# A pre-norm linear-attention and GEGLU block: nearly all matmuls as 64-row pairs, and a new order on every engine

## The chip, the cores and the metric

The kernel runs on one core of one Trainium2 chip. A core has TensorE (matmuls, from SBUF into the eight banks of PSUM), VectorE, ScalarE and GpSimd for elementwise work, and queues that issue transfers; here SyncE's queue (SP) issues nearly all of them, and ScalarE's the first three. The metric is the device time of one execution in microseconds, the median of several runs. A profile is one execution of its own; its span, from the first to the last instruction, is a little shorter than its time.

## The reference

All tensors are bf16; x has 2048 rows (tokens) of 448 values.

```python
def _A_ref(x, wqkv, wo):            # 16 heads of 28 values
    qkv = (x @ wqkv) ...            # wqkv: 448 x 1344
    phi = lambda t: jnp.where(t > 0, t + 1, jnp.exp(t)) + 1e-6
    pq, pk = phi(q), phi(k)
    kv = jnp.einsum("bhsd,bhse->bhde", pk, v)
    z = jnp.einsum("bhsd->bhd", pk)
    num = jnp.einsum("bhqd,bhde->bhqe", pq, kv)
    den = jnp.einsum("bhqd,bhd->bhq", pq, z)[..., None] + 1e-6
    return (num / den) ... @ wo     # wo: 448 x 448

h  = x + _A_ref(_layernorm(x), wqkv, wo)
n  = _layernorm(h)
h2 = h + (gelu(n @ w_gate) * (n @ w_up)) @ w_down    # 448 x 1792, 448 x 1792, 1792 x 448
```

The sums kv and z run over all tokens. So no output of attention can begin before the last token has been added, while Q needs only its own tokens.

## The kernel before, in words

**Tiles.** The 2048 tokens are 16 tiles of 128. The width of 448 is 3.5 times 128, or 7 times 64. A matmul takes a block of weights of up to 128 rows (the contracted dimension) and up to 128 columns, and streams up to 512 columns of data past it. It may also use only the upper or the lower 64 rows of the array; two such matmuls, one on each half, that write different PSUM banks form a pair.

**Stages and names.** Each task has a name and a number; the names return in the prediction.

- Warm-up: warm0 (38 matmuls on 128 rows), warm1 (8 pairs).
- First norm: for each tile statistics and aggregate (bnst, bnag) on VectorE, the inverse deviation on ScalarE (ln, rstd), the normalised rows (norm), on VectorE for tiles 0 and 1 and on GpSimd for the rest, there with a negated mean (negm). The rows are transposed into `xnT`: tiles 0 to 3 on TensorE (tr) with a copy from PSUM (ev), the others by transposing transfers (xT), for which ScalarE repeats the last 64 columns (dup).
- kv, per one or two tiles: k takes three 128-row matmuls, v takes three, and then v adds the last 64 rows of both as one pair. phi(k) is an exponential on ScalarE (ek), a clamp on GpSimd (cl) and a combination on VectorE (ph); v is copied by ScalarE (evv). acc adds four groups of 112 columns with a column of ones into one PSUM bank (`BK_ACC`). After the last tile VectorE masks the sum into `kvz` (kz1, kz2).
- Q: 16 groups, (four stretches of 512 tokens) x (four groups of 112 columns). qp takes four 128-row matmuls, of which the lower half of the last is zeros; then exponential (eq, ScalarE), clamp (cq, GpSimd) and combination from PSUM (pq, VectorE) into `pqT`.
- Attention's output, per tile: nd (four matmuls, 113 rows), reciprocal and product (rd, om) on VectorE, a transposition (tro and a copy evo for tiles 0 and 1, a transposing transfer oT for the others), wo, the residual and the second norm's statistics (hr, hbnst, hbnag) on VectorE, the norm (hln, hrstd, normh), a repetition of columns (wrap) and a transposition (trh and evh, or hT).
- GEGLU: gate/up groups gu0 to gu55, in chunks of 2, 2, 4, 4 and 4 tiles. Each is a run of 64-row pairs, gate on the upper rows into bank 0 or 1, up on the lower into bank 6 or 7. ScalarE applies the gelu (ge, two halves), VectorE multiplies (hm, two halves). down multiplies 14 blocks of 128 rows per tile; VectorE adds the residual (out) and a transfer stores it (dout).

**Order.** Nothing is scheduled at run time. `ORDERS` holds for TensorE, ScalarE, VectorE, GpSimd and SP one list of task names, and each engine works through its own list. A task that needs another engine's result, or a buffer that is still read, waits by semaphore; everything behind it in its list waits too. `_Graph.add` finds these dependences from the buffers that a task reads and writes, the PSUM banks among them; with `mw=True` a task places each wait in front of the matmul that needs it. In the lists, the last tasks of TensorE are down8 to down15; tile 15 is split in two halves of columns. Arguments such as `dur`, `lat`, `key` and the constants at the top served the search for an order and issue nothing.

The matmul of one Q group, and the end of v, read:

```python
for k in range(4):
    ins = e.matmul(psQ, wq_sb[:, k, g * GW:(g + 1) * GW], xnT[:, k, c * QCH:(c + 1) * QCH], start=(k == 0), stop=(k == 3))
...
ins = e.matmul(ps[:, BK_K[t % 4], 0:D], xnT[0:64, 3, t * 128:(t + 1) * 128], wt_sb[0:64, :], start=False, stop=True)
ins = e.matmul(ps[:, BK_V[t % 2], 0:D], xnT[64:128, 3, t * 128:(t + 1) * 128], wt_sb[64:128, :], start=False, stop=True)
```

Of the kernel before, what the change touches and what calls it, by code (L numbers as in the profile page):

```python
# [875 lines left out]
```

## Time and profile before

| | |
|---|---|
| median of 3 runs | 200.32 us (200.12 to 201.09) |
| the profiled execution | 200.7 us |
| its span | 199.0 us |
| TensorE's clock | 1.000 |
| busy: TensorE, VectorE, ScalarE, GpSimd | 97%, 60%, 36%, 25% of the span |

A line of a group names the source line, the engine, the operation, the tiles written and read, the shape (partitions x elements) and the count; then the busy time in us and the mean duration of one in ns; then the idle time before it and what ended it. In a timeline the first number is the start in us and the second the time from the first start to the last end of what is merged in the row. PE is TensorE, PEld its weight loads, DVE VectorE, ACT ScalarE, POOL GpSimd.

### The profile page before, as it was taken

Reading aid. Unit: us, or ns where it says so; the run is one execution under the profiler, and the core shown is the slowest. Engines: PE = TensorE matmul, PEld = TensorE weight load, DVE = VectorE, ACT = ScalarE, POOL = GpSimd, SP = SyncE. Lnnn points to the kernel's source line nnn. Section 1 sums busy time; section 2 is a strip of 40 time slices with the busy share of each in tenths; the row PEclk is TensorE's granted clock in tenths of the full one; section 3 lists DMA queues with packets and bytes.
Section 4 is the critical chain, followed back from the end, with each engine's and each line's share of the span. In section 5 each row is a group of like instructions: output and inputs, shape, how many; then the busy total and the mean of one; then the engine's idle time right before and its main releaser. Section 6 shows DMA issues by size and latency. Waiting matters only on the chain.

```text
span 199.0 us, 4435 instructions
## 1 busy us (share of the span) xinstructions
PE 193.8 (97%) x1698; PEld 113.6 (57%) x1698; DVE 119.5 (60%) x301; ACT 72.3 (36%) x203; POOL 50.6 (25%) x104
## 2 busy tenths in 40 slices
PE   7999999999998999999999999999999999999995
PEld 7544554566596865784454545665545455645554
DVE  3898434299999959497784877544513354442212
ACT  3487683665662330224310334344410243410000
POOL 2299973464315052241050235000000000000000
DMA  6974536996760532555226202700000100001111
GB/s 195 377 227 85 105 54 131 235 241 127 212 180 14 110 63 46 118 80 122 48 45 149 53 3 48 138 3 2 3 19 28 46 3 0 0 3 46 46 46 46
DMA packets 37172, 17.41 MB, mean 87 GB/s; under 512 B 28256, under 2 KB 36256, under 8 KB 37152
## 3 DMA queue, kind: packets, MB, share of 16 engines
q1 hardware_dynamic: 36272, 16.39, 34.8%
q10 hardware_dynamic: 880, 0.75, 1.2%
q8 instruction: 13, 0.21, 0.5%
q14 instruction: 7, 0.06, 0.1%
HBM read 8.66 MB, written 1.84 MB: 53 GB/s over the span
## 4 chain that ended last, share of the span: by engine, by line
PE 89%; DVE 4%; DMA 2%; ACT 2%; POOL 1%; issue 1%; DVEq 0%; POOLq 0%
PE ps L774 30%; PE ps L735 21%; PE ps L776 11%; PE ps L610 5%; PE ps L548 4%; PE ps L556 4%; PE ps L673 4%; DMA oT<-o_sb 2%; PE ps L440 2%; PE ps L585 2%; PE ps L634 2%; PE ps L559 2%; DVE pqT L615 1%; PE ps L674 1%; ACT xnT L527 1%; DVE o_sb L638 1%
## 5 line engine op out<-in xcount | busy, mean ns | idle before, releaser
L776 PE MATMUL ps<-hnT,wgu_sb 64*128 64x512 bf16 (+1 forms) x490 | 87.0, 334 | 0.0
L774 PE MATMUL ps<-hnT,wgu_sb 64*128 64x512 bf16 (+1 forms) x490 | 86.7, 333 | 0.0
L798 ACT ACTIVATE gl<-ps 128x256 bf16<-128x256 f32 x112 | 36.9, 381 | 82.1 <-PE ps L776 79.3
L800 DVE TENSOR_TENSOR hh<-ps,gl 128x256 bf16<-128x256 f32 x112 | 42.6, 418 | 28.5 <-ACT gl L798 26.1
L774 PEld LDWEIGHTS ps<-hnT,wgu_sb 64*128 64x128 bf16 x490 | 45.3, 94 | 20.9 <-issue 0.7
L776 PEld LDWEIGHTS ps<-hnT,wgu_sb 64*128 64x128 bf16 x490 | 43.9, 94 | 9.9 <-DVE hh L800 2.9
L735 PE MATMUL ps<-wd_sb,hh 128*128 128x448 bf16 (+1 forms) x238 | 43.3, 342 | 0.0
L735 PEld LDWEIGHTS ps<-wd_sb,hh 128*128 128x128 bf16 x238 | 22.9, 98 | 19.5 <-issue 1.0
L740 DVE TENSOR_TENSOR x_sb<-ps,x_sb 128x448 bf16<-128x448 f32 (+1 forms) x17 | 10.1, 594 | 24.2 <-PE ps L735 24.2
L456 DVE BATCH_NORM_STATS2 st<-x_sb 128x6 f32<-128x448 bf16 x32 | 18.8, 613 | 2.4 <-DMA x_sb<-in_A_x_dram 2.3
L577 DVE SCALAR_TENSOR_TENSOR pk<-ps,tm 128x448 bf16<-128x448 f32 x16 | 9.3, 621 | 11.2 <-POOL tm L575 9.6
L610 PE MATMUL ps<-xnT,wq_sb 128*112 128x512 bf16 x64 | 15.9, 380 | 0.0
L614 POOL TENSOR_SCALAR tm<-e 112x512 bf16<-112x512 bf16 x16 | 9.9, 621 | 9.2 <-ACT e L613 7.3
L615 DVE SCALAR_TENSOR_TENSOR pqT<-ps,tm 112x512 bf16<-112x512 f32 x16 | 10.7, 681 | 1.8 <-POOL tm L614 1.8
L613 ACT ACTIVATE e<-ps 112x512 bf16<-112x512 f32 x16 | 9.6, 600 | 4.7 <-PE ps L610 4.4
L548 PE MATMUL ps<-wkv_sb,xnT 128*128 128x448 bf16 x48 | 10.6, 353 | 0.2 <-ACT xnT L527 0.2
L575 POOL TENSOR_SCALAR tm<-e 128x448 bf16<-128x448 bf16 x16 | 8.8, 561 | 7.4 <-ACT e L574 7.4
L684 DVE TENSOR_TENSOR x_sb<-ps,x_sb 128x448 bf16<-128x448 f32 x16 | 9.4, 619 | 2.1 <-PE ps L675 2.1
L556 PE MATMUL ps<-wkv_sb,xnT 128*128 128x448 bf16 x48 | 10.6, 353 | 0.0
L698 POOL TENSOR_SCALAR hn<-x_sb,nm,rs 128x448 bf16<-128x448 bf16 x14 | 10.3, 745 | 0.8
L579 ACT ACTIVATE v<-ps 128x448 bf16<-128x448 f32 x16 | 8.7, 551 | 4.9 <-PE ps L560 4.9
L473 POOL TENSOR_SCALAR ln<-mv 128x2 f32<-128x2 f32 x7 | 1.5, 220 | 33.7 <-DVE mv L457 33.4
(76 smaller groups left out, 159.0 us busy)
## 6 DMA issues: line engine op xcount, KB each, us to landing
out_dram<-x_sb SPq DMA_DIRECT2D x15, 112.0 KB, 1.7
wgu_sb<-in_B_w_gate_dram SPq DMA_DIRECT2D x7, 224.0 KB, 5.0
wgu_sb<-in_B_w_up_dram SPq DMA_DIRECT2D x7, 224.0 KB, 5.3
wd_sb<-in_B_w_down_dram SPq DMA_DIRECT2D x1, 1568.0 KB, 7.1
x_sb<-in_A_x_dram SPq DMA_DIRECT2D x2, 448.0 KB, 5.3
wkv_sb<-in_A_wqkv_dram ACTq DMA_DIRECT2D x2, 336.0 KB, 3.7
x_sb<-in_A_x_dram SPq DMA_DIRECT2D x3, 224.0 KB, 4.3
wo_sb<-in_A_wo_dram SPq DMA_DIRECT2D x2, 336.0 KB, 5.7
```

What stands on the lines that cost most here:

```text
L456: op("dve", lambda e: e.bn_stats(st[:, t, :], src_ap), [b_src], [b_st[t]], "%sbnst%d" % ("" if mv is mv1 else "h", t), 0.53, key, after=after)
L548: ins = e.matmul(ps[:, BK_K[t % 4], 0:D], xnT[:, k, t * 128:(t + 1) * 128], wkv_sb[:, k, 0:D], start=(k == 0), stop=False)
L556: ins = e.matmul(ps[:, BK_V[t % 2], 0:D], xnT[:, k, t * 128:(t + 1) * 128], wkv_sb[:, k, D:2 * D], start=(k == 0), stop=False)
L610: ins = e.matmul(psQ, wq_sb[:, k, g * GW:(g + 1) * GW], xnT[:, k, c * QCH:(c + 1) * QCH], start=(k == 0), stop=(k == 3))
L615: op("dve", lambda e, i=i, c=c, g=g, psQ=psQ: e.scalar_tensor_tensor(pqT[0:GW, g, c * QCH:(c + 1) * QCH], psQ, EPS, tm2[:, i, :], ALU.max, ...
L698: op("pool", lambda e, t=t, sh=sh: e.tensor_scalar(hn[:, sh, 0:D], h_sb[:, t, :], nm2[:, t:t + 1], rs2[:, t:t + 1], ALU.add, ALU.mult), [b ...
L735: ins = e.matmul(psO, hh[:, j, (t % HR) * 128:(t % HR + 1) * 128], wd_sb[:, j, c0:c1], start=(j == 0), stop=(j == NJ - 1))
L740: op("dve", lambda e, t=t, psO=psO, c0=c0, c1=c1: e.tensor_tensor(x_sb[:, t, c0:c1], psO, h_sb[:, t, c0:c1], ALU.add), bank(bk) + [b_h[t]] ...
L774: e.matmul(psG[:, jj * N:(jj + 1) * N], wgu_sb[A_, k, j * 128:(j + 1) * 128], hnT[A_, ka_, c0:c0 + N], start=(k == 0), stop=(k == 6))
L776: ins = e.matmul(psU[:, jj * N:(jj + 1) * N], wgu_sb[B_, k, j * 128:(j + 1) * 128], hnT[B_, kb_, c0:c0 + N], start=(k == 0), stop=(k == 6))
L798: G.add("act", lambda e, gi=gi, cs_=cs_, psG=psG: e.activation(gl[:, gi, cs_], psG[:, cs_], AF.Gelu_apprx_tanh), r=bank(BK_G[i]), w=[b_glh ...
L800: op("dve", lambda e, dst=dst, srcU=srcU, srcL=srcL: e.tensor_tensor(dst, srcU, srcL, ALU.mult), bank(BK_U[i]) + [b_glh], [b_ar[j_][t % HR ...
```

## The change

1. k, v, Q, wo of tiles 2 to 15, nd of tiles 2 to 15, down of tiles 0 to 11, the kv sum and the transposes tr0 to tr3 become pairs of 64-row matmuls. With seven blocks of 64 rows for each of two outputs, the first task takes four blocks of the one output on the upper rows and four of the other on the lower, and the second task the remaining three of each, with the halves exchanged. The names become k and v, qa and qb, and a suffix a and b.
2. The second task of such a couple writes each bank from the other half of the array. `_Graph.add` now leaves out the semaphore between two tasks of TensorE that write a bank from the same half (`rg`), and keeps it where the half differs.
3. Q's weights get 16 columns of zeros behind them and a second copy of the last 64 rows (one more transfer, dwq_u), pk's groups are padded from 113 to 128 columns; the weights of a matmul are then 128 columns wide.
4. The kv sum lies in two banks, each written by both halves.
5. The last eight Q groups (two stretches of 512 tokens): ScalarE writes the exponential into `pqT` and copies Q itself into the freed `xn` (rq). Clamp and combination follow later, from SBUF and in place.
6. Norms 2 and 3 move to VectorE; GpSimd's norms subtract the mean themselves, and negm goes.
7. The banks of k, v and Q come from tables, and all five lists are new. warm1 stands ahead of warm0; down8 to down11 stand among the last gate/up groups.

```diff
 ORDERS = (
-    "warm0 tr0 warm1 k0 tr1 v0 k1 v1 tr2 tr3 k2 qp0 v2 acc0 acc1 qp1 k4 v4 qp2 acc2 k6 acc3 v6 acc4 k8 acc5 v8 qp3"
-    " acc6 k10 acc7 v10 acc8 k12 acc9 v12 acc10 k14 acc11 v14 acc12 qp4 acc13 qp5 acc14 qp6 acc15 qp7 qp8 nd0 nd1 qp9"
-    " qp10 nd2 tro0 nd3 tro1 qp11 wo0 wo1 qp13 qp12 qp15 wo2 trh1 trh0 qp14 nd5 nd4 gu0 gu1 gu2 gu3 wo4 gu4 nd7 nd6"
-    " gu5 gu6 gu7 gu8 wo6 down1 nd9 nd8 down0 gu9 gu10 wo8 gu11 nd10 nd11 gu12 gu13 gu14 gu15 gu16 gu17 wo10 gu18 gu19"
-    " nd12 nd13 down3 down2 wo12 gu21 nd15 nd14 gu20 gu23 gu22 gu25 wo14 gu24 gu27 gu26 gu29 gu28 gu31 gu30 gu33 gu32"
...
+    "warm1 warm0 tr0 tr1 k0 v0 tr2 k1 tr3 v1 acc0a k2 k3 v2 v3 qa00 acc0b acc1b qb00 k4 acc1a acc2a v4 k5 acc2b acc3b"
+    " v5 k6 qa01 v6 qb01 k7 acc3a acc4a v7 k8 acc4b acc5b v8 acc5a k9 acc6a qa10 v9 qb10 k10 acc6b acc7b v10 k11 acc7a"
+    " acc8a v11 acc8b k12 qa11 v12 acc9b qb11 k13 acc9a acc10a v13 k14 acc10b acc11b v14 k15 acc11a acc12a v15 acc12b"
+    " acc13b qa20 acc13a acc14a qb20 acc14b acc15b acc15a qa21 nd1 nd0 qb21 qa30 nd2a tro0 nd2b tro1 wo0 wo1 qb30 qa31"
+    " qb31 trh0 trh1 wo2a wo2b gu0 nd4a gu1 nd4b gu2 gu3 gu4 gu5 wo4a wo4b gu6 nd6a gu7 nd6b gu8 down0a gu9 wo6a gu10"
+    " wo6b gu11 down0b nd8a gu13 nd8b gu12 down2a gu15 gu14 wo8a gu17 wo8b gu16 nd10a down2b nd10b gu19 gu18 gu21 gu20"
+    " wo10a wo10b gu23 nd12a gu22 nd12b gu25 gu24 gu27 gu26 down4a wo12a down4b wo12b gu29 nd14a gu28 nd14b gu31 gu30"
+    " down6a gu32 wo14a gu33 wo14b gu34 down6b gu35 gu36 gu37 gu38 gu39 gu40 gu41 gu42 gu43 gu44 gu45 gu46 gu47 gu48"
+    " down8a gu49 gu50 down8b gu52 gu51 gu54 down10a gu53 down10b gu55 down12 down13 down14 down15 down15b",
...
+    " ek12 evv12 eq6 eq7 ek13 ek14 evv13 evv14 ek15 evv15 rq8 eq8 rq9 eq9 rq11 eq10 evo0 rq10 evo1 eq11 rq12 hln0"
+    " hrstd0 hln1 hrstd1 eq14 evh0 eq12 eq13 eq15 rq13 tbl2 ge0_1 ge0_0 rq15 rq14 ge1_0 ge1_1 ge2_0 ge2_1 ge3_0 ge3_1"
...
+    " pq6 pq7 ph13 ph14 ph15 kz2 kz1 rd1 rd0 om1 om0 pq8 rd2 rd3 om2 om3 hr0 hbnst0 hr1 hbnag0 hbnst1 hbnag1 normh0"
+    " wrap0 normh1 wrap1 evh1 hr3 hr2 hbnst3 hbnst2 hm0_0 hbnag3 hm0_1 hbnag2 rd4 hm1_0 hm1_1 om4 rd5 om5 hm2_0 hm2_1"
+    " hm3_0 wrap2 hm3_1 hm4_0 wrap3 pq11 hm4_1 pq13 hm5_0 hm5_1 hr4 hr5 hbnst4 hbnst5 hbnag4 hm6_0 hbnag5 hm6_1 rd6"
+    " om6 rd7 om7 pq10 pq9 hm7_1 wrap4 hm7_0 hm8_1 pq15 wrap5 hm8_0 pq14 hm9_0 hm9_1 hr6 hr7 hbnst7 hbnst6 hbnag7"
+    " hm11_1 hbnag6 pq12 hm10_1 hm11_0 hm10_0 wrap7 out1 wrap6 out0 rd8 hm13_1 hm13_0 rd9 om8 om9 hm12_1 hm12_0 hm15_1"
...
 class _Graph:
...
         def dep(d, k):
             if d is None or d is t:
+                return
+            if d.eng == "pe" and eng == "pe" and all(d.rg.get(b, g) == g for b, g in t.rg.items()):
+                if d not in t.odeps:
+                    t.odeps.append(d)
+                    d.succ.append(t)
                 return
...
+        def pairs(mms, waits):
+            def fn(e, W):
+                ins = None
+                for n, (o_, l_, r_, s_, p_, kw) in enumerate(mms):
+                    if n in waits:
+                        W(n)
+                    ins = e.matmul(o_, l_, r_, start=s_, stop=p_, **kw)
+                return ins
+            return fn
...
+        def kv_tile(t):
...
+            a1 = [kmm(s, oK, 0, s == 0, False) for s in (0, 2, 4, 6)]
+            b1 = [kmm(s, oV, 1, s == 1, False) for s in (1, 3, 5, 6)]
+            a2 = [kmm(s, oV, 1, False, s == 4) for s in (0, 2, 4)]
+            b2 = [kmm(s, oK, 0, False, s == 5) for s in (1, 3, 5)]
+            pe_pairs("k%d" % t, both(a1, b1), D, [b_xnT[t], b_wk, (b_wv, 1), (b_wkt, 6), (b_wvt, 7)], [(b_ps[bk], 0), (b_ps[bv], 1)], kk, {bk: "A", bv: "B"})
+            pe_pairs("v%d" % t, both(a2, b2), D, [b_xnT[t], b_wk, b_wv], bank(bk, bv), kk + 0.5, {bk: "B", bv: "A"})
...
+                        lst.append(mm(ps[:, BK_X + g // 2, (g % 2) * 256:(g % 2) * 256 + GP], pk[rows, i, g, :], v1[rows, i, g, :],
+                                      t == 0 and n == 0 and not flip, t == T - 1, skip_group_check=True))
+                x, y = ("B", "A") if flip else ("A", "B")
+                acc_tasks.append(pe_pairs(name, both(a, b), GP, [b_pk[i], b_v1[i]], bank(BK_X, BK_Y), kk - 5.0, {BK_X: x, BK_Y: y}))
...
+        def q_pair(c, h):
...
+            pe_pairs("qa%d%d" % (c, h), both(a1, b1), QCH, rx, [(b_ps[p_], 0), (b_ps[q_], 1)], kq, {p_: "A", q_: "B"}, after=acc_tasks[-1:] if n_ >= Q_LATE else ())
+            pe_pairs("qb%d%d" % (c, h), both(a2, b2), QCH, rx, bank(p_, q_), kq + 0.5, {p_: "B", q_: "A"})
...
+                    act_exp(lambda e, pq_=pq_, psQ=psQ: e.activation(pq_, psQ, AF.Exp), bank(banks[n]), [b_pqT[g][c]], "eq%d" % q, _c_act(QCH), kq)
+                    op("act", lambda e, qs=qs, psQ=psQ: e.activation(qs, psQ, AF.Identity), bank(banks[n]), [b_xn[sl], b_xnd[sl]], "rq%d" % q, _c_act(QCH), kq)
+                    op("pool", lambda e, pq_=pq_: e.tensor_scalar(pq_, pq_, 1.0 + EPS, 0.0, ALU.min, ALU.max), [b_pqT[g][c]], [b_pqT[g][c]], "cq%d" % q, 0.58, 60.0 + q)
+                    op("dve", lambda e, pq_=pq_, qs=qs: e.scalar_tensor_tensor(pq_, qs, EPS, pq_, ALU.max, ALU.add),
+                       [b_xn[sl], b_pqT[g][c]], [b_pqT[g][c]], "pq%d" % q, _c_dve(QCH), 60.0 + q)
...
+        def a2_pair(t):
...
+            pe_pairs("nd%da" % t, both(ndmm(t, P, 0), ndmm(t + 1, Q, 1)), 116, rq, [(b_ps[P], 0), (b_ps[Q], 1)], ka, {P: "A", Q: "B"})
+            pe_pairs("nd%db" % t, both(ndmm(t + 1, Q, 0), ndmm(t, P, 1)), 116, rq, bank(P, Q), ka + 0.1, {P: "B", Q: "A"})
...
+            pe_pairs("wo%da" % t, both(a1, b1), D, [b_oT[e0], (b_oT[e1_], 1)] + b_wo, [(b_ps[P], 0), (b_ps[Q], 1)], ka + 4, {P: "A", Q: "B"})
+            pe_pairs("wo%db" % t, both(a2, b2), D, [b_oT[e0], b_oT[e1_]] + b_wo, bank(P, Q), ka + 4.1, {P: "B", Q: "A"})
...
+        def down_pair(t, key):
+            P, Q = BK_O
+            for n, (ta, tb, oa, ob) in enumerate(((t, t + 1, P, Q), (t + 1, t, Q, P))):
+                a = [mm(ps[:, oa, 0:D], hh[A_, j, hsl(ta)], wd_sb[A_, j, :], n == 0 and j == 0, n == 1 and j == NJ - 1) for j in range(NJ)]
+                b = [mm(ps[:, ob, 0:D], hh[B_, j, hsl(tb)], wd_sb[B_, j, :], n == 0 and j == 0, n == 1 and j == NJ - 1) for j in range(NJ)]
```

More of the change, by code (lines that the diff above doesn't have):

```diff
@@ L404, in bass_sequential_preLN__linear_attn_block__glu_gated_geglu__prompt_kernel, with dma_x @@
[L404 to L405 removed]
+        def dma_x(a, b):
+            dma(x_sb[:, a:b, :], xv[:, a:b, :], b_x[a:b], "dx%d" % a, (b - a) * 128 * D * 2, first=True)
+        dma_x(0, 1)
+        dma_x(1, 2)
+        dma(wkv_sb[:, 0:3, 0:D], krows(A_wqkv, 0, 384, D, 2 * D), [b_wk], "dwk", 384 * D * 2, q="act", first=True)
@@ L608, in fnq @@
                 ins = None
                 for k in range(4):
-                    ins = e.matmul(psQ, wq_sb[:, k, g * GW:(g + 1) * GW], xnT[:, k, c * QCH:(c + 1) * QCH], start=(k == 0), stop=(k == 3))
+                    ins = e.transpose(tvo[:, k, :], o_sb[:, so, k * 128:(k + 1) * 128], ident[:])
                 return ins
-            G.add("pe", fnq, r=[b_xnT[t] for t in tiles] + b_wq, w=bank(bq), name="qp%d" % q, dur=_c_mm(QCH, 4), lat=PE_L, key=kq)
-            act_exp(lambda e, i=i, psQ=psQ: e.activation(e2[:, i, :], psQ, AF.Exp), bank(bq), [b_e2[i]], "eq%d" % q, _c_act(QCH), kq)
@@ new lines, in a2_first, with ftrh @@
+            tvh = psb[:, bh, 0:896].rearrange("p (k t) -> p k t", k=7)
+            def ftrh(e):
+                ins = None
+                for k in (0, 1, 2, 4, 5, 6, 3):
+                    ko = k * 128 if k < 4 else (k - 4) * 128 + 64
+                    ins = e.transpose(tvh[:, k, :], hn[:, sh, ko:ko + 128], ident[:])
+                return ins
+            G.add("pe", ftrh, r=[b_hn[sh], b_hnd[sh], b_ident], w=bank(bh), name="trh%d" % t, dur=_c_mm(128, 7), key=ka)
+            hv_ = hnT[:, :, (t % HR) * 128:(t % HR + 1) * 128]
```

664 lines of the change are left out of this document (308 added, 356 removed), and 72 rows, old and new, of the table ORDERS.

## The prediction

> **What bounds the kernel now.** I read the page's busy shares first, then the chain that ended last, then a table of stretches, and last the order of time on TensorE around its seams.
>
> ```profile
> span 199.0 us, 4435 instructions
> PE 193.8 (97%) x1698; PEld 113.6 (57%) x1698; DVE 119.5 (60%) x301; ACT 72.3 (36%) x203; POOL 50.6 (25%) x104
> PE 89%; DVE 4%; DMA 2%; ACT 2%; POOL 1%; issue 1%; DVEq 0%; POOLq 0%
> ```
>
> TensorE is busy for 97% of the span and makes 89% of the chain. A busy PE still hides time here, because one matmul's busy interval overlaps the next; so I read distances from start to start. The stretches (from the span's start) show whether another engine could bind:
>
> ```profile
> core 0: us, PE busy (x) PEld busy (x) DVE busy (x) ACT busy (x) POOL busy (x), PEclk, DMA share, GB/s
> 17.20:41.80 24.60, 24.60 (x174) 13.11 (x172) 11.93 (x24) 16.16 (x43) 16.21 (x31) 1.00 0.63 137
> 41.80:55.35 13.55, 13.39 (x100) 8.34 (x97) 13.47 (x32) 8.09 (x17) 5.69 (x10) 1.00 0.81 195
> 55.35:89.60 34.25, 33.47 (x470) 25.34 (x472) 27.52 (x74) 10.06 (x28) 10.64 (x21) 1.00 0.41 82
> 122.00:196.60 74.60, 74.48 (x574) 41.30 (x568) 29.62 (x73) 18.95 (x58) 1.67 (x3) 1.00 0.12 31
> ```
>
> The clock is full (1.00). In the second stretch, from the last kv sum to the first gate/up group, VectorE is as full as TensorE (13.47 of 13.55 us). In the third it has 27.52 of 34.25. Everywhere else only TensorE binds. What TensorE loses is seen at its seams:
>
> ```profile
> 33.71 0.73 PE L556 MATMUL ps<-wkv_sb,xnT 128*128 128x448 bf16 x3
> 34.38 0.36 PE L559 MATMUL ps<-wt_sb,xnT 64*128 64x448 bf16 x1
> ...
> 34.58 0.35 PE L559 MATMUL ps<-wt_sb,xnT 64*128 64x448 bf16 x1
> ...
> 34.86 0.42 PE L585 MATMUL ps<-v,pk 128*113 128x113 bf16 x4
> ...
> 35.84 0.57 PE ps L548 x3
> 36.41 0.21 PE ps L585 x4
> 36.62 1.13 PE ps L556 x6
> ...
> 38.59 0.86 PE ps L610 x4
> ```
>
> Six 448-column matmuls take 1.13 us, 0.189 each. The last of the three at 33.71 therefore gives way at 34.28, but the first 64-row matmul starts at 34.38: 0.10 lost. The second 64-row pair started at 34.58, could give way at 34.77, and the 128-row kv sum starts at 34.86: 0.09 lost. So a change of row mode costs about 0.096 us each way. In the order of TensorE the 64-row work stands in 23 separate runs (the warm-up pairs, nine v tails, seven output-projection tails and gate/up groups in between), so 46 changes, 4.4 us. The waits for other engines are few:
>
> ```profile
> PE ps L440 <- POOL mhalf L413: 1.4, 1, 1.4
> PE ps L673 <- DMA oT<-o_sb: 0.8, 1, 0.8
> PE ps L548 <- ACT xnT L527: 0.2, 1, 0.2
> PE ps L708 <- DVE hn L701: 0.2, 1, 0.2
> ```
>
> The last three make 1.2 us; the first, 1.4 us, is the wait before the first warm-up matmul, which stays.
>
> **The change part by part.**
>
> *Row modes.* After the change 128-row work remains in the warm-up, the first two tiles of attention (nd0, nd1, tro, wo, trh) and the last four down tiles. Counting runs in the new order (warm1; tr0 to qa21; qb21 to nd2a; nd2b; the tail of wo0; the tail of wo1 to qb31; wo2a to gu55) gives 7 runs, the first at the very start: 13 changes. That is 33 fewer: 33 x 0.096 = -3.2 us.
>
> *Does a pair cost what a 128-row matmul costs?* The 64-row pairs that exist answer it:
>
> ```profile
> 64.00 0.27 PE L774 MATMUL ps<-hnT,wgu_sb 64*128 64x256 bf16 x1
> 64.01 0.27 PE L776 MATMUL ps<-hnT,wgu_sb 64*128 64x256 bf16 x1
> 64.11 0.27 PE L774 MATMUL ps<-hnT,wgu_sb 64*128 64x256 bf16 x1
> ...
> 6.68 0.21 PE L448 MATMUL ps<-ones_bf 64*128 64x116 bf16 x1
> ...
> 6.73 0.21 PE L448 MATMUL ps<-ones_bf 64*128 64x116 bf16 x1
> ```
>
> Both halves of a pair start within 0.01 us, and the next pair follows after 0.11 us at 256 columns and 0.05 us at 116; four kv-sum matmuls took 0.21, the same 0.05. So twice the matmuls and weight loads in the same slots: k and v (7 slots a tile before and after), wo from tile 2 (7 a pair of tiles), down (14 a tile), nd and the kv sum (4 a tile) cost nothing more. Their weight loads are covered as those of gate/up are now.
>
> *Q.* Before, a group of 112 columns took four slots, the fourth half zeros: 0.86 us by the row at 38.59, 0.216 a slot. Two groups as pairs share 7 slots instead of 8: 8 pairs of groups x 0.216 = -1.7 us. Padding weights to 128 columns I count as nothing: the loads of 112 columns lie beside 0.216 us slots already.
>
> *Hand-overs.* New is that the second half of every pair task (k then v, qa then qb, a then b) writes each PSUM bank from the other row half, and waits by semaphore until the first has drained. The trace has no such wait; its parts are there:
>
> ```profile
> L674 PE MATMUL ps<-wo_sb,oT 64*128 64x448 bf16 x7 | 2.5, 360 | 0.0
> 52.76 0.29 DVE L701 COPY hn<-hn 128x64 bf16<-128x64 bf16 x2
> 53.11 0.95 PE L708 MATMUL ps<-ident,hn 128*128 128x128 bf16 x14 [0.16 <-DVE hn L701]
> ```
>
> A pair lasts 0.360 of which 0.189 is its slot, so 0.17 remains, and from an end on VectorE (53.05) to the matmul it frees (53.11) are 0.06: about 0.23 us where a and b stand next to each other. Bounds: 0, if something covers it, and 0.23. In the new order most have another task between (nd between gate/up groups, two kv sums between k and v, one gate/up between halves of wo). Bare are six: k0/v0, acc15b/acc15a, qa31/qb31, and wo2, wo4, wo10: 6 x 0.22 = +1.3 us.
>
> The Trainium skill, TensorEngine Tiling (Array Packing), Gotcha 1: PSUM Pressure, says that different row tiles cannot access the same PSUM bank simultaneously and that software must synchronise. No run here shows the conflict, since no bank of this trace is written by both row halves in turn; by the rule all 60 second halves need the guard, covered or not, and the sum for those six is the same.
>
> *Start.* The first kv pair now needs the V weights beside the K weights.
>
> ```profile
> 6.93 0.74 PE L548 MATMUL ps<-wkv_sb,xnT 128*128 128x448 bf16 x3
> 7.51 0.33 PE L518 MATMUL ps<-ident,xn 128*128 128x128 bf16 x3
> ...
> 7.95 0.74 PE L556 MATMUL ps<-wkv_sb,xnT 128*128 128x448 bf16 x3
> ```
>
> Three K matmuls ran from 6.93 to 7.51 while V was on its way; they move behind 7.95: +0.6 us. The transposes tr0 to tr3, now ten small ones each, lie partly in that gap; bounds -0.3 and +0.3, taken as 0. Norms 2 and 3 move from GpSimd to VectorE and all 15 negations leave GpSimd; one more 56 KB weight load stands on SP's queue ahead of the transposes of xn, which wait there for the norms anyway:
>
> ```profile
> SPq L529 <- ACT ln L466: 3.8, 2, 2.6
> ```
>
> All taken as 0: in the kv stretch VectorE has 11.93 and GpSimd 16.21 of 24.60 us. If that cover were gone, k4 would wait for its transpose.
>
> *The last eight Q groups.*
>
> ```profile
> L613 ACT ACTIVATE e<-ps 112x512 bf16<-112x512 f32 x16 | 9.6, 600 | 4.7 <-PE ps L610 4.4
> L615 DVE SCALAR_TENSOR_TENSOR pqT<-ps,tm 112x512 bf16<-112x512 f32 x16 | 10.7, 681 | 1.8 <-POOL tm L614 1.8
> L800 DVE TENSOR_TENSOR hh<-ps,gl 128x256 bf16<-128x256 f32 x112 | 42.6, 418 | 28.5 <-ACT gl L798 26.1 <-PE ps L735 2.0
> L684 DVE TENSOR_TENSOR x_sb<-ps,x_sb 128x448 bf16<-128x448 f32 x16 | 9.4, 619 | 2.1 <-PE ps L675 2.1
> L718 DVE COPY hn<-hn 128x448 bf16<-128x448 bf16 x14 | 4.3, 313 | 4.2 <-POOL hn L698 4.2
> L817 ACT ACT_TABLE_LOAD x1 | 1.3, 1283 | 0.0
> L798 ACT ACTIVATE gl<-ps 128x256 bf16<-128x256 f32 x112 | 36.9, 381 | 82.1 <-PE ps L776 79.3 <-DVE hn L718 1.8 <-DVE pqT L615 1.0
> ...
> 51.84 0.99 DVE L695 TENSOR_SCALAR hn<-x_sb,mv,rs 128x448 bf16<-128x448 bf16 x2
> ```
>
> ScalarE gets eight more activations, 8 x 0.60 = 4.8 us; six of them stand before the first gate/up group (8.09 + 3.6 of 13.55 us: they fit, but rq12 stands ahead of hln0). VectorE loses six or seven of its pq from the stretch where it is full, 6 x 0.68 = 4.1 us; the first gate/up group can start earlier, which only lets TensorE's saving through. The price comes later: pq9 to pq15 stand between the multiplications of gate/up, whose U bank is double, so a late multiplication stops the group after next. Taking pq from SBUF is priced between the copy, 0.31, and 0.68; I take 0.68. From the end of gu4 to the start of gu8 TensorE has gu5, wo4, gu6, nd6, gu7: 3 x 1.53 + 1.5 + 0.4 = 6.5 us. VectorE has six multiplications, a copy, two pq, and hr, statistics and aggregates of two tiles: 2.5 + 0.3 + 1.4 + 1.2 + 1.2 + 0.3 = 6.9, about 0.5 late. Two more such walks. From the end of wo1 to trh0, TensorE has ten Q slots and a hand-over, 2.4 us, and VectorE hr, two statistics (as hr), two aggregates and a wrap (0.15 each) and a norm, 0.62 x 3 + 0.45 + 0.5 = 2.8: 0.4 late. From the end of evh0, TensorE reaches gu2 after wo2 with its hand-over, gu0, nd4 and gu1, 1.5 - 0.4 (trh1) + 3.1 + 0.4 = 4.6 us; ScalarE has four Q activations issued every 0.5, the table load and two gelus, 2.0 + 1.3 + 0.8, and VectorE two multiplications, 0.8: 4.9, so 0.3 late. Together +1.2. Bounds: 0, and seven pq wholly exposed, 4.8.
>
> *Old waits.* The 0.8 us for oT goes, since wo4 stands behind gu5 instead of gu3 (3 us later) and needs the transposes no earlier; the two of 0.2 lie in the reordered part: -1.2. Late next could be hT3 before gu7: its copy stands behind hm4_0, with gu5, wo4 and gu6 (4.6 us) left to land; I count nothing.
>
> *The end.* Tiles 8 to 11 of down move in among the gate/up groups, where their inputs are long ready; down12 to 15 stay last and cover the last multiplication as down8 does now. 0.
>
> Sum: -3.2 - 1.7 + 1.3 + 0.6 + 1.2 - 1.2 = -3.0. The profiled execution took 200.7 us around its span of 199.0; 200.7 - 3.0 = 197.7. It stands 0.4 over the median of the runs, 200.32, so the median after is 197.3.
>
> **The rivals.** *No new costs:* the order hides hand-overs and VectorE's queue. For it: TensorE idles 0.12 us in all in the last 74.6 us now. Then -3.2 - 1.7 - 1.2 + 0.6 = -5.5, so 194.8. Against: six bare hand-overs can be read in the order.
> *VectorE becomes the bound in gate/up:* all seven moved pq are exposed, 4.8 instead of 0.5: 197.3 + 4.3 = 201.6 at worst, 200.2 if two thirds are. For it: 27.52 of 34.25 us are busy and 2 to 3 us come on top; against: down0 and nd stand there too as cover. It cancels the gain from 3.0 us of exposure beyond what is counted.
> *Slower: a swap of row halves in a bank stops the array as a mode change does*, though another task stands between. Place: the 60 second halves (16 v, 16 kv sums, 8 qb, 7 nd, 7 wo, 6 down). Price: the 54 not yet counted x 0.096 = 5.2, so 202.5. It turns the sign from 0.056 each. For it: Gotcha 1, as above, is about just this; against: nothing in the trace, and gate/up changes banks from group to group without a gap, though never the half. That the pairs do not run side by side is excluded by the rows at 64.00.
>
> **How the numbers follow.** No change that a measurement of this kernel can tell is within 0.5%, 199.3 to 201.3. My forecast, 0.64, by itself 195.6 to 199.0; no new costs 0.16; VectorE bound 0.11; swap stalls 0.09. Faster: 0.64 + 0.16 = 0.80. Same: most of VectorE's rival, 0.10. Slower: swap stalls and VectorE's worst, 0.10. The range from 194.6 to 200.4 leaves out the swap case, the upper part of VectorE's, and a little below.
>
> **What would show it.** Right: changes of row mode leave 13 gaps of 0.1 us; Q slots 56 of 0.216; the first gate/up group starts near 53.5 us instead of 55.3; from gu8 on the lead grows by about 1.7 us in small steps; bare hand-overs show gaps of 0.2 us. Wrong would make it: gaps of TensorE on hh in gate/up, gaps at covered swaps, hT landing after gu7 is due, kv sums waiting for pk.

## The result, and the profile after

| | before | after |
|---|---|---|
| median of 4 runs | 200.49 us (200.12 to 201.09) | 218.21 us (217.97 to 218.33) |
| the profiled execution; its span | 200.7 us; 199.0 us | 217.97 us; 216.2 us |
| ratio of after to before | | 1.0879, 95% interval 1.0849 to 1.0909 |

The change makes the kernel 17.7 us slower; 197.3 us was forecast. TensorE's clock is no part of it: the profiled execution took 217.97 us at a granted clock of 1.000, the other three 218.11 to 218.33 us at 0.984. The first lines of the page after, the busy digits of two engines in 40 equal slices, and the shares of the chain that ended last:

```profile
span 216.2 us, 5358 instructions
PE 194.8 (90%) x2192; PEld 112.0 (52%) x2192; DVE 119.3 (55%) x303; ACT 77.2 (36%) x211; POOL 76.3 (35%) x87
...
PE   8895748599999799797999998999998999999995
...
POOL 2189999943322907126006153026062000000000
...
PE 51%; POOL 24%; DVE 13%; issue 5%; ACT 4%; DMA 2%; POOLq 1%; SPq 0%; DVEq 0%; ACTq 0%
```

TensorE's share of the chain falls from 89% to 51%, and GpSimd's rises from 1% to 24%. GpSimd has 17 instructions fewer than before (87, not 104) and yet 25.7 us more work (76.3, not 50.6). The groups of GpSimd by shape name the work; first after, then before:

```profile
L481 POOL TENSOR_SCALAR hn<-x_sb,mv,rs 128x448 bf16<-128x448 bf16 x14 | 26.7, 1914 | 0.8 <-POOL rs L477 0.2
L481 POOL TENSOR_SCALAR xn<-x_sb,mv,rs 128x448 bf16<-128x448 bf16 x12 | 22.3, 1860 | 1.3 <-DVE st L463 1.3
```

```profile
L698 POOL TENSOR_SCALAR hn<-x_sb,nm,rs 128x448 bf16<-128x448 bf16 x14 | 10.3, 745 | 0.8
L496 POOL TENSOR_SCALAR xn<-x_sb,nm,rs 128x448 bf16<-128x448 bf16 x14 | 9.9, 718 | 0.4 <-ACT rs L468 0.2
```

The same engine, shape, type and operation name, and yet one norm takes 1.86 to 1.91 us in place of 0.72 to 0.75. In the code, it added a negated mean and then multiplied; now it subtracts the mean and then multiplies. Where this time gets onto the path, the waits tell (us in total, times, longest):

```profile
DVE pk L560 <- POOL tm L558: 20.2, 11, 3.4
...
DVE hn L737 <- POOL hn L481: 10.9, 9, 1.9
...
PE ps L431 <- DVE pk L560: 7.7, 5, 2.3
...
PE ps L431 <- DVE hh L820: 5.5, 7, 1.5
```

They belong to two stages, with two mechanisms. The table of stretches shows the kv stage (first row) and gate/up's beginning (third row):

```profile
core 0: us, PE busy (x) PEld busy (x) DVE busy (x) ACT busy (x) POOL busy (x), PEclk, DMA share, GB/s
17.20:52.20 35.00, 25.91 (x307) 13.75 (x306) 15.67 (x31) 18.89 (x51) 29.54 (x34) 1.00 0.41 89
52.20:65.40 13.20, 12.92 (x137) 6.30 (x137) 9.19 (x23) 9.28 (x21) 3.62 (x6) 1.00 0.70 157
65.40:109.00 43.60, 38.88 (x594) 29.66 (x596) 29.07 (x76) 13.93 (x38) 16.68 (x15) 1.00 0.41 90
```

**kv stage: GpSimd is full.** It has 29.54 us of work, in a stage that lasted 24.60 before, and until shortly after its last norm it hardly pauses, with 25.77 of 26.10 us (columns as above):

```profile
17.20:43.30 26.10, 17.05 (x192) 8.78 (x193) 10.86 (x24) 13.59 (x40) 25.77 (x27) 1.00 0.27 52
```

The clamps of phi(k) stand between the norms in its list, so each comes late, and with it phi(k), which empties the bank of K. The end of this full part in the chain (start, us, what), and then the row of TensorE where it ends, from the timeline:

```profile
36.13 1.86 POOL xn L481
...
39.06 1.86 POOL xn L481
40.93 0.54 POOL tm L558
...
41.59 0.64 DVE pk L560
...
42.27 2.80 PE ps L431 x33
```

```profile
42.27 0.74 PE L431 MATMUL ps<-wkv_sb,xnT 64*128 64x448 bf16 x5 [1.05 <-DVE pk L560]
```

The clamp (tm) runs directly behind a norm, phi(k) behind the clamp, and TensorE goes on 0.04 us later, after 1.05 us of idling. What waits there are matmuls of K and V: their bank is still to be read by phi(k) of an earlier tile. All five waits on pk are of this kind.

**Gate/up: GpSimd is not full (16.68 of 43.60 us), but one norm lies in a chain.** First rows of VectorE's timeline (start, duration, what ended the idle time before), then the row of TensorE's that follows:

```profile
73.36 0.42 DVE L820 TENSOR_TENSOR hh<-ps,gl 128x256 bf16<-128x256 f32 x1 [0.54 <-ACT gl L818]
75.39 0.28 DVE L737 COPY hn<-hn 128x448 bf16<-128x448 bf16 x1 [1.61 <-POOL hn L481]
75.58 0.75 DVE L820 TENSOR_TENSOR hh<-ps,gl 128x256 bf16<-128x256 f32 x2
```

```profile
76.06 1.70 PE L431 MATMUL ps<-hnT,wgu_sb 64*128 64x256 bf16 x27 [1.48 <-DVE hh L820]
```

VectorE stands 1.61 us at the column repetition (wrap, L737) until GpSimd's norm is there. Behind it in VectorE's list stand products hh of gate/up, which hold the banks that the next group writes. So TensorE idles 1.48 us, "on hh", though VectorE had time to spare. The like returns with later tiles, seven times in all by the row above.

How much of the 17.7 us is from each stage needs a kernel without the slow norm. That is the first experiment.

### The profile page after: what moved, and what is told of

Read it like the earlier page. It is cut to its first block, busy times and chain, and to the rows that moved or that the text cites. A ratio compares the mean times of both kernels' runs of the same rounds, so it can differ in the third digit from the quotient of the medians.

```text
span 216.2 us, 5358 instructions
## 1 busy us (share of the span) xinstructions
PE 194.8 (90%) x2192; PEld 112.0 (52%) x2192; DVE 119.3 (55%) x303; ACT 77.2 (36%) x211; POOL 76.3 (35%) x87
## 4 chain that ended last, share of the span: by engine, by line
PE 51%; POOL 24%; DVE 13%; issue 5%; ACT 4%; DMA 2%; POOLq 1%; SPq 0%; DVEq 0%; ACTq 0%
PE ps L431 45%; POOL hn L481 10%; POOL xn L481 8%; PE ps L768 5%; DVE hh L820 4%; DVE st L463 3%; DVE x_sb L649 2%; POOL rs L477 2%; DMA x_sb<-in_A_x_dram 2%; POOL tm L558 1%; ACT pqT L613 1%; DVE mv L464 1%; POOLq L260 1%; POOL ln L475 1%; POOL tm L606 1%
## 5 line engine op out<-in xcount | busy, mean ns | idle before, releaser
L431 PE MATMUL ps<-hnT,wgu_sb 64*128 64x512 bf16 (+1 forms) x980 | 93.9, 333 | 5.0 <-DVE hh L820 5.0
L431 PEld LDWEIGHTS ps<-hnT,wgu_sb 64*128 64x128 bf16 x980 | 48.8, 94 | 43.1 <-DVE hh L820 11.6
L431 PE MATMUL ps<-wd_sb,hh 64*128 64x448 bf16 x336 | 35.7, 349 | 2.0 <-DVE x_sb L744 1.5
L431 PE MATMUL ps<-wkv_sb,xnT 64*128 64x448 bf16 x192 | 25.4, 351 | 9.5 <-DVE pk L560 7.7
L431 PEld LDWEIGHTS ps<-wd_sb,hh 64*128 64x128 bf16 x336 | 20.1, 94 | 13.9 <-DVE x_sb L744 1.8
L481 POOL TENSOR_SCALAR hn<-x_sb,mv,rs 128x448 bf16<-128x448 bf16 x14 | 26.7, 1914 | 0.8 <-POOL rs L477 0.2
L481 POOL TENSOR_SCALAR xn<-x_sb,mv,rs 128x448 bf16<-128x448 bf16 x12 | 22.3, 1860 | 1.3 <-DVE st L463 1.3
L431 PE MATMUL ps<-xnT,wq_sb 64*128 64x512 bf16 x112 | 15.7, 377 | 0.3
L431 PE MATMUL ps<-wo_sb,oT 64*128 64x448 bf16 x98 | 12.8, 350 | 0.2
L768 PE MATMUL ps<-wd_sb,hh 128*128 128x448 bf16 (+1 forms) x70 | 10.8, 315 | 0.0
L737 DVE COPY hn<-hn 128x448 bf16<-128x448 bf16 x14 | 4.0, 286 | 10.9 <-POOL hn L481 10.9
```

Of the source, the lines that this page charges most:

```text
L431: ins = e.matmul(o_, l_, r_, start=s_, stop=p_, **kw)
L481: return lambda e: e.tensor_scalar(dst, src[:, t, :], mv[:, t, 0:1], rs[:, t:t + 1], ALU.subtract, ALU.mult)
L768: ins = e.matmul(ps[:, bk, c0:c1], hh[:, j, hsl(t)], wd_sb[:, j, c0:c1], start=(j == 0), stop=(j == NJ - 1))
```

## The experiments

"After" and "before" are the two kernels; the ratio is always to before, on the same chip.

**1. Only the norm's operation put back.** GpSimd negates the means again (13 short instructions) and adds:

```diff
-    op("pool", norm(u, hn[:, sh, 0:D], h_sb, mv2, rs2), ...)            # subtract, mult
+    negm(list(tt), mv2, nm2, b_mv2, b_nm2, ka)                          # nm = -1 * mean
+    op("pool", pnorm(u, hn[:, sh, 0:D], h_sb, nm2, rs2), ...)           # add, mult
```

> The changed kernel, with GpSimd's 26 norms written as before: negate the mean (12 small instructions more on GpSimd), then add and multiply, in place of subtract and multiply. All pairs, banks and orders stay as changed. Theory N (the subtracting norm on GpSimd, 1.86 to 1.91 us in place of 0.72, is the whole loss): each norm back at 0.72 to 0.75 us, GpSimd busy near 50 us instead of 76, and 195 to 199 us, the prediction without its sign error. Theory P (64-row pairs, their hand-overs and the new order cost the time): 214 us or more, since only GpSimd gets faster. Both at work: 203 to 210.

Measured: 199.82 us, ratio 0.9948 (0.9919 to 0.9978). Groups and stretches of this kernel (columns as above):

```profile
L485 POOL TENSOR_SCALAR hn<-x_sb,nm,rs 128x448 bf16<-128x448 bf16 x14 | 10.6, 766 | 0.8 <-POOL rs L476 0.2
...
L485 POOL TENSOR_SCALAR xn<-x_sb,nm,rs 128x448 bf16<-128x448 bf16 x12 | 8.6, 718 | 1.6 <-ACT rs L469 0.8 <-ACT xn L530 0.2 <-ACT e L566 0.2
```

```profile
17.20:41.50 24.30, 23.76 (x301) 14.45 (x297) 14.15 (x28) 17.26 (x46) 17.86 (x33) 1.00 0.61 108
41.50:54.50 13.00, 12.77 (x137) 6.36 (x137) 9.19 (x23) 9.09 (x21) 3.63 (x6) 1.00 0.96 185
54.50:90.00 35.50, 35.19 (x564) 28.90 (x564) 28.24 (x73) 12.89 (x35) 10.49 (x18) 1.00 0.47 103
```

All of the loss is gone, and a little more, though the time stays 0.8 us above the 195 to 199 expected. Pairs, new orders and the late Q groups are all still in, so none of them makes the loss without the subtraction. The kv stage takes 24.30 us in place of 35.00 and the beginning of gate/up 35.50 in place of 43.60; the middle stretch is nearly the same (13.00 and 13.20).

**2. Only the norm's operation changed, in the kernel before.** The negations stay, though nothing uses them:

```diff
-    ... tensor_scalar(xn[:, sl, 0:D], x_sb[:, t, :], nm1[:, t:t + 1], rs1[:, t:t + 1], ALU.add, ALU.mult)
+    ... tensor_scalar(xn[:, sl, 0:D], x_sb[:, t, :], mv1[:, t, 0:1], rs1[:, t:t + 1], ALU.subtract, ALU.mult)
```

(the second norm likewise).

> The kernel before, its GpSimd norms (14 of the first norm, 14 of the second) changed to subtract the mean and multiply, read from where the statistics leave it; the negations stay, nothing else moves. Theory N: 1.86 to 1.91 us a norm, and 212 to 220 us, as slow as the changed kernel. Theory P: 200 to 202 us. If the old order has more room for GpSimd than the new one: 204 to 211.

Measured: 225.90 us, ratio 1.1239 (1.1201 to 1.1277).

```profile
L698 POOL TENSOR_SCALAR hn<-x_sb,mv,rs 128x448 bf16<-128x448 bf16 x14 | 26.6, 1908 | 0.8
L496 POOL TENSOR_SCALAR xn<-x_sb,mv,rs 128x448 bf16<-128x448 bf16 x14 | 26.1, 1870 | 0.2 <-ACT ln L466 0.2
```

It takes no pair and no new order to lose this time. The old order loses more, 25.2 us, and more than any of the expected ranges. Two more norms are on GpSimd there, and the negations too; the profiled execution also had a mean granted clock of 0.970, not 1.000. How much each of these makes was not taken apart.

**3 and 4. The operation, or the place of its operand?** Together with the operation, the change moved the mean from a column of its own (`nm`) to one of two columns that alternate (`mv`). Experiment 3 is after with the mean copied to its own tile, still subtracting. Experiment 4 is after with the mean read from `mv`, but added; the sign of the mean is then wrong, so only its time is read.

```diff
 # 3
+    nm = 1.0 * mean            # copied, not negated
+    tensor_scalar(dst, src[:, t, :], nm[:, t:t + 1], rs[:, t:t + 1], ALU.subtract, ALU.mult)
 # 4
-    tensor_scalar(dst, src[:, t, :], mv[:, t, 0:1], rs[:, t:t + 1], ALU.subtract, ALU.mult)
+    tensor_scalar(dst, src[:, t, :], mv[:, t, 0:1], rs[:, t:t + 1], ALU.add, ALU.mult)
```

> As the changed kernel, but GpSimd first copies the means into a tile of their own (multiply by 1.0, the same small instruction as the negation), and the norm subtracts that copy. If the operation subtract is slow: norms of 1.86 to 1.91 us and 216 to 220 us. If the place of the operand is slow (every second word of the statistics): norms of 0.72 to 0.75 us and the time of the adding kernel, 195 to 199.

> As the changed kernel, but GpSimd's norms add the mean, read in place from the statistics, instead of subtracting it (the sign of the mean is wrong for 12 tiles of the first norm and 14 of the second, everything else is as in the reference). If the operation is slow: norms of 0.72 to 0.75 us and 195 to 199 us. If the place of the operand is slow: norms of 1.86 to 1.91 us and 216 to 219 us.

Measured: 222.11 us for 3 and 198.74 us for 4, each a single run without an interval. The second norm among the groups, of 3 and then of 4:

```profile
L485 POOL TENSOR_SCALAR hn<-x_sb,nm,rs 128x448 bf16<-128x448 bf16 x14 | 26.5, 1898 | 0.8 <-POOL rs L476 0.2
```

```profile
L484 POOL TENSOR_SCALAR hn<-x_sb,mv,rs 128x448 bf16<-128x448 bf16 x14 | 10.1, 727 | 0.8 <-POOL rs L477 0.2
```

The operand's place doesn't change the duration of a norm. The pair of operations alone decides between 0.73 and 1.90 us. Experiment 4 differs from after in this alone, and its span is 19.2 us shorter (197.0 and 216.2). Experiment 3 lies above its expected 216 to 220 us; it has 13 copies of 0.27 us more on GpSimd than after, 3.5 us of the same full engine, which may be why.

**5. Which pairs are slow?** In the kernel of experiment 1, each of the twelve first norms on GpSimd gets another form, so its output is not the reference's and its total time says nothing. Each form is one instruction of one execution.

```diff
+    s1, s2, o1, o2 = {4: (nm, rs, ALU.add, ALU.mult), 5: (nm, rs, ALU.subtract, ALU.mult),
+        6: (rs, nm, ALU.mult, ALU.add), 7: (rs, nm, ALU.mult, ALU.subtract), 8: (nm, None, ALU.subtract, None),
+        9: (nm, None, ALU.add, None), 10: (0.01, 1.5, ALU.subtract, ALU.mult), 11: (0.01, 1.5, ALU.add, ALU.mult),
+        12: (0.01, None, ALU.subtract, None), 13: (nm, rs, ALU.max, ALU.mult), 14: (rs, nm, ALU.mult, ALU.max),
+        15: (nm, rs, ALU.add, ALU.add)}[t]
```

> The changed kernel with the adding norm, in which GpSimd's twelve norms of the first layer norm each use another form of the same instruction (128 x 448, bf16 to bf16), so that the output is not the reference's: tile 4 add then multiply, 5 subtract then multiply, 6 multiply then add, 7 multiply then subtract, 8 subtract alone, 9 add alone, 10 and 11 subtract or add and multiply with constants, 12 subtract of a constant alone, 13 maximum then multiply, 14 multiply then maximum, 15 add twice. If any subtract is slow: 5, 7, 8, 10 and 12 take 1.86 to 1.91 us, the rest 0.55 to 0.75. If only subtract in the first place with a value per partition is slow: 5 and 8 alone. If only forms made of add and multiply are fast: 13 and 14 are slow too.

Rows of GpSimd's timeline (start, duration): tile 4 (add, mult), 5 (subtract, mult), 6 (mult, add), 8 (subtract alone), 9 (add alone), 11 (add, mult with constants) and 15 (add, add):

```profile
11.74 0.71 POOL L496 TENSOR_SCALAR xn<-x_sb,nm,rs 128x448 bf16<-128x448 bf16 x1 [0.75 <-ACT rs L469]
...
12.96 1.88 POOL L496 TENSOR_SCALAR xn<-x_sb,nm,rs 128x448 bf16<-128x448 bf16 x1
...
17.61 0.71 POOL L496 TENSOR_SCALAR xn<-x_sb,rs,nm 128x448 bf16<-128x448 bf16 x1
...
19.20 1.40 POOL L496 TENSOR_SCALAR xn<-x_sb,nm 128x448 bf16<-128x448 bf16 x1 [0.17 <-ACT v L582]
...
22.27 1.41 POOL L496 TENSOR_SCALAR xn<-x_sb,nm 128x448 bf16<-128x448 bf16 x1
...
32.21 0.56 POOL L496 TENSOR_SCALAR xn<-x_sb 128x448 bf16<-128x448 bf16 x1
...
33.17 1.88 POOL L496 TENSOR_SCALAR xn<-x_sb,nm,rs 128x448 bf16<-128x448 bf16 x1 [0.18 <-POOL nm L481]
```

The others: mult, subtract 1.86; max, mult 1.86; mult, max 1.87; subtract, mult with constants 1.72; subtract of a constant alone 1.34. So subtraction is not the slow case. Addition and multiplication together, in either order, are a fast one, as is the clamp (min, max with constants), at 0.56; every other form tried takes 1.3 to 1.9, a lone addition among them. That the single addition is twice as slow as addition and multiplication together none of the three theories had foreseen. What makes these pairs fast, the runs don't show.

**6. Do the losses of the two stages add up?** The kernel of experiment 1, with only the second norm subtracting:

```diff
-    op("pool", pnorm(u, hn[:, sh, 0:D], h_sb, nm2, rs2), ...)
+    op("pool", norm(u, hn[:, sh, 0:D], h_sb, mv2, rs2), ...)
```

> The changed kernel with the adding norm in the first layer norm and the subtracting one in the second (14 norms of 1.9 us), negations on GpSimd as in the adding kernel. By the two traces TensorE lost 8 us more up to the first gate/up groups and 10 us more behind them in the changed kernel than in the adding one. If the two stages lose independently: 199.8 + 10 = 208 to 211 us. If one late stage hides the other: either below 203 or above 214.

Measured: 208.35 us, ratio 1.0380 (1.0343 to 1.0417). Against experiment 1 that is 0.0432 x 200.8 = 8.7 us for the second norm. From there to after are 1.0879 - 1.0380 = 0.0499, so 10.0 us for the first norm. That the two make the whole 18.7 us against experiment 1 is so by construction; whether the stages lose independently, the start of the first gate/up group tells, in after and then in this kernel (first start, us):

```profile
66.01 1.25 PE L431 MATMUL ps<-hnT,wgu_sb 64*128 64x256 bf16 x20
```

```profile
54.92 1.26 PE L430 MATMUL ps<-hnT,wgu_sb 64*128 64x256 bf16 x20
```

In experiment 1 this group starts at 55.27 us. So in after 10.7 of the 18.1 us between the spans (216.2 and 198.1) are lost up to there and 7.4 behind it, not 8 and 10 as expected above. The second norm alone loses nothing up to there and 8.7 us behind it (span 206.4). The stages lose nearly independently: 10.7 and 8.7 would be 19.4, and both together lose 18.1. The first norm alone was not run.

**7. The price of a change of row mode.** The kernel of experiment 1 with tiles 0 to 11 of down in the old form, 14 matmuls of 128 rows a tile, in the same places of the order; 24 more changes of mode.

```diff
-    down_pair(t, kd)
+    down_wide(t, kd)      # per tile: for j in range(14): matmul(ps[BK_O[n]], hh[:, j, tile], wd_sb[:, j, :], start=(j == 0), stop=(j == 13))
```

> The changed kernel with the adding norm (199.82 us by the median), down of tiles 0 to 11 back to 128-row matmuls, tile by tile, at the places of the halves a and b. Nothing else moves. This puts 12 runs of 128 rows between 64-row work, 24 more changes of row mode. If a change costs 0.096 us wherever it stands: 24 x 0.096 = 2.3 us, 202.1 us. If the mode-change term of the prediction was wrong (changes hide in a full stream, or pairs cost as much in their place): 199.3 to 200.3.

Measured: 201.32 us, ratio 1.0027 (1.0012 to 1.0043), 0.0079 x 200.8 = 1.6 us over experiment 1. The time lies between the two expectations. The span of the profiled execution is 2.4 us longer (200.5, not 198.1), but this execution was slower than the median and has other new waits (TensorE waits 1.4 us for transposing transfers, not 0.4). Changes between down and gate/up leave gaps of 0.09 to 0.11 us in its trace, so the price of one holds. Whether all of 24 x 0.096 = 2.3 us arrives in the time can't be told: by the two intervals the difference is 0.9 to 2.3 us. The Trainium skill, TensorEngine Tiling (Array Packing), Key Properties, says that a change of tiling mode drains TensorE, without a price; the trace shows the gap of about 0.1 us, and not whether the array is empty in it.

**8. The negation on VectorE.** The 13 negations take 13 x 0.256 = 3.3 us of GpSimd in experiment 1; here VectorE does them, each behind the aggregate that it needs.

```diff
-            op("pool", lambda e: e.tensor_scalar(nm[:, a:b], mv[:, a:b, 0], -1.0, None, ALU.mult),
+            op("dve", lambda e: e.tensor_scalar(nm[:, a:b], mv[:, a:b, 0], -1.0, None, ALU.mult),
```

> The changed kernel with the adding norm, but VectorE negates the mean, in a small instruction right behind the aggregates, instead of GpSimd. If GpSimd's queue with the negations in it holds up the kv stage and the second norm: the 198.7 us that the run without negations showed, give or take 0.5. If VectorE is as short of time: 199.8 or more.

Measured: 199.43 us, ratio 0.9930 (0.9913 to 0.9947), the fastest kernel of this study that computes everything, 1.4 us under before. Its interval overlaps that of experiment 1, and it lies between the two expectations, so it doesn't decide between them.

**9 to 11. Covering the bare hand-overs by hand.** All start from experiment 8. Number 9 puts another task into four of the six, 10 into one of them, 11 into three, with two attention tasks moved one gate/up group later so that they don't meet their banks occupied, and VectorE's list moved to suit.

```diff
 # 9
-    ... wo1 qb30 qa31 qb31 trh0 trh1 wo2a wo2b ... wo4a wo4b gu6 nd6a ... wo10a wo10b gu23 nd12a
+    ... wo1 qa31 qb30 qb31 wo2a trh0 trh1 wo2b ... wo4a gu6 wo4b nd6a ... wo10a gu23 wo10b nd12a
 # 10
-    ... wo1 qb30 qa31 qb31
+    ... wo1 qa31 qb30 qb31
 # 11: as 10, and
-    ... wo4a wo4b gu6 nd6a gu7 nd6b gu8 ... wo10a wo10b gu23 nd12a gu22 nd12b gu25
+    ... wo4a gu6 wo4b gu7 nd6a gu8 nd6b ... wo10a gu23 wo10b gu22 nd12a gu25 nd12b
```

> As the one that negates on VectorE, and four of the six bare hand-overs get another task between their halves: gu6 between wo4a and wo4b, gu23 between wo10a and wo10b, the transposes trh between wo2a and wo2b, qb30 between qa31 and qb31. If a bare hand-over is worth its gap (0.22 to 0.24 us in the traces): 4 x 0.22 = 0.9 us below that kernel, near 197.8. If TensorE's gaps there stand in for waits that come anyway: no difference within 0.3.

> The kernel that negates on VectorE (199.43 us), with qb30 moved between qa31 and qb31 and nothing else. If a bare hand-over costs its gap: 199.2, 0.23 us less, at the edge of what can be told. If the swap delays what waits for qb30 (its two groups on ScalarE, and behind them the second norm's first activation): 199.6 to 201.

> As the last one, and wo4 and wo10 get a gate/up group between their halves, as in the run that took 204.2 us, but now nd6 and nd12 stand one gate/up group later and VectorE multiplies before it adds the residuals, so that PSUM banks 4 and 5 are read before nd asks for them. If that run lost to the banks (two gaps of 0.88 and two of 0.48 us) and to the transposes held behind wo2a: 198.6 to 199.3. If any change of this order costs time elsewhere: 200 or more.

Measured: 204.20 us, ratio 1.0157 (1.0137 to 1.0176) for 9; 200.24, 0.9971 (0.9954 to 0.9989) for 10; 207.07, 1.0306 (1.0257 to 1.0354) for 11. All three are slower than experiment 8, where 0.2 to 0.9 us had been to gain: 10 and 11 as their slower alternatives said, 9 outside both of its own. The largest waits of TensorE in 9 and in 11 that experiment 8 has not, or has only for 0.4 us in all (oT):

```profile
PE ps L414 <- DVE x_sb L642: 2.1, 4, 0.7
```

```profile
PE ps L392 <- DMA oT<-o_sb: 3.1, 3, 1.6
...
PE ps L662 <- DVE hn L655: 1.1, 1, 1.1
```

In 9, the attention of the next tiles waits for the residual (hr, L642) to leave its bank, since one gate/up group of cover is gone from between. In 11 that wait shrinks to 0.6 us, and the transposes of the attention output come late instead. The wait of 1.1 us for the rows of the second norm (hn) is in 10 too, and not in experiment 8. Each cover was to save 0.22 us, and each set of swaps lost more than it could save. The waits named do not make up the whole of the 4.8 and 7.6 us over experiment 8; the rest was not taken apart.

**12. The late Q groups without the split.** Experiment 8 with the last eight Q groups taken from PSUM as the first eight are. Their VectorE work had to move forward in its list, between tiles 0 to 3 of attention, so this tests the split together with the place it allows.

```diff
-    SPLIT = cfg.get("split", (4, 5, 6, 7))
+    SPLIT = ()
-    ... pq8 rd2 rd3 om2 om3 hr0 ... (pq9 to pq15 between the hm of gate/up)
+    ... pq8 pq9 rd2 rd3 om2 om3 pq10 hr0 pq11 ... pq12 hr3 pq13 hr2 ... pq14 ... pq15
```

> The kernel that negates on VectorE (199.43 us), with the last eight Q groups as before: no copy on ScalarE, combination on VectorE from PSUM, its eight instructions moved forward in VectorE's list to where the banks are needed. If the split takes VectorE's load out of the stretch where it is full and this sets the first gate/up group: 2 to 4 us slower, 201.5 to 203.5. If TensorE has no other work in that stretch anyway, or the later combinations cost as much: 198.9 to 200.

Measured: 204.69 us, ratio 1.0207 (1.0177 to 1.0237), that is 0.0277 x 200.8 = 5.6 us over experiment 8, or 3.7 us by the spans of the profiled executions (201.4 and 197.7).

```profile
PE ps L392 <- DVE pqT L578: 1.9, 3, 1.2
```

This is slower than both expectations. TensorE waits for pq, three times, where it had no such wait: without the split and in this order, VectorE doesn't empty the banks of Q in time. The 1.9 us are about half of the difference between the spans; the rest, and how much of it is the changed order, was not taken apart.

## Why the prediction was wrong

**The step that failed** is "Norms 2 and 3 move from GpSimd to VectorE and all 15 negations leave GpSimd ... All taken as 0: in the kv stretch VectorE has 11.93 and GpSimd 16.21 of 24.60 us." It counted the instructions that leave GpSimd and gave the norms that stay their old duration, without pricing that these had changed from add, mult to subtract, mult: 26 norms by 1.14 to 1.17 us, 30 us of new work on GpSimd. Experiments 1 and 2 show that this alone makes the loss, in either kernel, and 3 and 4 that it is the operation.

No row of the trace before gave the 1.9 us: GpSimd's norms took the 0.72 and 0.75 us above. But the trace before gave the point from which it decides, and that was not worked out. From 11.4 to 41.5 us, where twelve of its norms of the first layer norm stand, GpSimd was busy for 21.48 of 30.10 us:

```profile
11.40:41.50 30.10, 29.71 (x204) 15.69 (x203) 17.06 (x39) 20.88 (x60) 21.48 (x41) 1.00 0.61 134
```

So 8.6 us were free, about 9.7 without the five negations there: from 0.8 us longer each on, twelve norms fill it. They became 1.14 us longer, 13.7 us in all. And every second norm lies in the chain from the residual to gate/up whatever the busy share is. An instruction whose operation is new on its engine belonged into the range as an unknown price, and into the rivals as the slower case. The three rivals were all about TensorE and VectorE.

The next sentence was: "If that cover were gone, k4 would wait for its transpose." Of the signs named for being wrong, "gaps of TensorE on hh in gate/up" are in the trace (5.5 us), and so are waits for pk (7.7 us), though of K's and V's matmuls for a bank and not of the kv sums. That the first sign came is luck: it belongs to the rival in which VectorE is the bound, and here it was GpSimd that made VectorE late.

**The other steps** can be judged on experiment 1, which has all of the change but the subtraction, and 13 negations on GpSimd that the change had taken away. I take as lost the distance from start to start beyond a matmul's slot (0.189 us for 448 columns, others in proportion), less 0.096 a change of mode and 0.23 a bare hand-over; the stretches are cut at 10, 40 and 55 us. The sums are good to about 0.2 us.

| step | predicted, us | in experiment 1, us |
|---|---|---|
| changes of row mode | -3.2 (46 to 13) | -3.2 (46 to 13) |
| slots, Q among them | -1.7 | -2.2 |
| six bare hand-overs | +1.3 | +1.4 |
| start | +0.6 | +0.7 (1.0 lost, but begun 0.3 earlier) |
| new waits less old ones | +1.2 - 1.2 = 0.0 | +2.4: kv stage 1.1, up to the first gate/up 0.9, behind it 0.4 |
| sum | -3.0 | -0.9 (spans 199.0 and 198.1) |

*Row modes, pairs and hand-overs* were right in kind and size. The start, from TensorE's timeline in experiment 1, has the first of the six; from 26.56 us on it has covered ones:

```profile
8.12 0.37 PE L430 MATMUL ps<-wt_sb,xnT 64*128 64x448 bf16 x2
8.55 0.74 PE L430 MATMUL ps<-wkv_sb,xnT 64*128 64x448 bf16 x6
...
26.56 0.73 PE L430 MATMUL ps<-wkv_sb,xnT 64*128 64x448 bf16 x6
27.13 0.35 PE L430 MATMUL ps<-wt_sb,xnT 64*128 64x448 bf16 x2
27.32 0.27 PE L430 MATMUL ps<-v,pk 64*128 64x113 bf16 x4
27.42 1.02 PE L430 MATMUL ps<-xnT,wq_sb 64*128 64x512 bf16 x8
28.28 0.73 PE L430 MATMUL ps<-wkv_sb,xnT 64*128 64x448 bf16 x6
```

From 8.12 to 8.55 are 0.43 us, one slot of 0.19 and 0.24 of hand-over. The others, at 43.34, 51.28, 54.28, 65.74 and 106.72 us, are 0.22 to 0.24: the six places that the order had shown. From 26.56 on, the halves of k, v and the kv sum change from row to row without a gap (three slots of 0.19, one, two of 0.05, four of 0.215). So the rival by which every swap of halves costs as much as a change of mode is out. The Trainium skill, TensorEngine Tiling (Array Packing), Gotcha 1: PSUM Pressure, only asks that software keeps two row tiles out of one bank at the same time, and its rule agrees with this: the price falls where the guard is bare.

*VectorE as the bound in gate/up* is out too: 28.24 of 35.50 us, and with GpSimd's norm put right the waits of TensorE on hh are 0.2 us, where 0.5 had been set for gu8 alone. *No new costs* is out by the hand-overs.

*The waits* were the mis-sized term: the 1.2 us that vanish were counted against 1.2 us of new ones, and 2.4 us more came than went. In the kv stage three gaps of 0.28 to 0.38 us (at 19.45, 24.33 and 32.67) make nearly all of the 1.1, for which the prediction had put 0; with the negations off GpSimd (experiment 8) this stage loses 0.2 us less. Experiment 4, which has no negations at all, has a span 1.1 us shorter than experiment 1 (197.0, one execution), so up to about that much of the 2.4 us may be theirs. The first gate/up group starts at 55.27 us, and not near 53.5. Had the operation stayed the same, the forecast would still have been 1.4 to 2.5 us too good (198.74 us in experiment 4, a single run, 199.82 in experiment 1). Its range (from 194.6 to 200.4) would have held; of the 3.0 us of gain, experiment 1 shows 0.9 and experiment 4 2.0, each against before on its chip.
